# Constants built by GpSimd, and idle matmuls in more TensorE gaps, in an attention and mixer kernel

## The chip, the cores and the metric

The kernel runs on one core of a Trainium2 chip, in one launch. The metric is the device time of that launch in microseconds (us). The engines are TensorE (PE, with its weight loads shown apart as PEld), VectorE (DVE), ScalarE (ACT), GpSimd (POOL) and SyncE (SP, which here only issues transfers). Matmul results land in PSUM, which has eight banks; everything else lives in SBUF.

## What is computed

The inputs are q, k and v of 4 batches, 8 heads, 768 positions and 64 features, and four weight matrices. The attention is block-sparse: keys are split into 12 blocks of 64, each query takes the three best blocks by a gate (query times mean key of the block) and its own block, under a causal mask. A token and channel mixer follows.

```python
k_rep = k.reshape(B, H, n_blocks, block, D).mean(axis=3)
gate_scores = np.einsum('bhsd,bhnd->bhsn', q, k_rep)
gate_scores = np.where(causal, gate_scores, -1000000000.0)
top_idx = np.argsort(gate_scores, axis=-1)[..., -top_k:]
...
scores = scale * np.matmul(q, k.transpose(0, 1, 3, 2))
mask = mask & (pos[:, None] >= pos[None, :])
scores = np.where(mask, scores, -1000000000.0)
...
return np.matmul(attn, v).astype(np.float32)
...
h = np.maximum(xt @ w_tok1, 0.0) @ w_tok2
u = x + h.transpose(0, 2, 1)
h2 = np.maximum(u @ w_ch1, 0.0) @ w_ch2
return (u + h2).astype(np.float32)
```

## The kernel before

The 32 heads are handled as 16 pairs; a pair `i` is one batch and two neighbouring heads `x` = 0 and 1. For each pair `prepare(i)` loads k and q (L312, two transfers each on SP's queue), transposes them on TensorE against a float32 identity `ident32` (L356, tiles `tkl` and `tql`), and writes the fp16 operands `KA` and `QA` of the score matmul. Most of these casts run on GpSimd (`cast`, L376); those of pair 0 run on ScalarE (`direct` L385, `qact` L390). VectorE sums the keys of a block (`ksum` L395, `kcopy` L403), TensorE makes the gate scores (`gate`, L413, ten matmuls, tile `gps`), VectorE picks the best three (`gm`, `top`, `below`, `bias`, L452 to L498), and the resulting mask is transposed back (`mask`, L500) and copied into 24 more rows of `QA` (`put_mask`, L509).

The mask reaches the scores without an operation of its own: rows 64 to 87 of `KA` hold an indicator, a 1 where a key column belongs to block n of head x, so that the score matmul over 88 rows adds the penalty that stands in the same rows of `QA`. The indicator is a constant. Ring slot 0 of `KA` gets it by a transfer on ScalarE's queue (L969), the other four slots by one transfer on GpSimd's queue (`more_ind`, L337).

`attend(i)` (L817) then runs, for each head, three groups of score matmuls (`scores`, L516, tile `sps`), the exponentials on ScalarE (`expo`, L534), the causal diagonal, the product with V (`av`, L550, 21 matmuls into the tile `aps`), and on VectorE the reciprocal of the row sums (`recip`, L562) and the scaling into `x16` (`norm`, L570). The causal diagonal of pair 0 is added on TensorE, by a matmul of `ident16` with a triangle `tri` (L530); of all other pairs VectorE multiplies by a 0/1 triangle `m0` (`diag`, L542). `tri` is made from `m0` by GpSimd (`make_tri`, L341), and `m0` and `ident32` come by transfer (L970, L947). PSUM is shared out as two tiles of two banks (ring `big`: transposes and scores), three single banks (ring `bank`) and one bank for the product with V (ring `av`). When the four pairs of a batch are through, its mixer follows (`tok1`, `umix`, `ch1`, `ch2`), mixed in between the attention of later pairs.

The order of the work is made by a planner. Every piece is an `Op` with an engine, an estimated occupancy and duration, its dependencies, a priority and the buffers it takes. `plan` (L118) goes forward in planned time, gives each engine the ready piece of best priority among those that can start within 60 ns of the earliest, and returns one list; the program issues the pieces in this order, and each engine runs its share strictly in it. The planner's start times per engine are in `free` (L121). The framework adds the semaphore waits that the data call for. Those for PSUM go by bank: two engines are kept apart in one bank even where their columns differ or both only read.

Idle matmuls are pieces like others (`dummy`, L706): a matmul of a zero tile `warm` on itself, without dependencies, with the worst priority (IDLE). The planner puts one wherever TensorE would otherwise wait, as long as planned time has not passed `WARM_END` (17,000 ns) and the `WARM` = 120 of them are not used up. They are 256 columns wide, are planned at 213 ns for the first `COLD` = 20 and 109 ns after, and write a tile that holds the slot of the ring `av`.

What stands ahead of the planned list: VectorE clears `warm`, ScalarE loads the exponential and starts the transfer of `ident32`, VectorE casts it to `ident16` and clears tiles, GpSimd sets the ones in V, starts the transfer of `m0` and clears the tiles `bn` (L944 to L972).

Of the kernel before, what the change touches and what calls it, by code (L numbers as in the profile page):

```python
# [9 lines left out]
FP = mybir.dt.float32  # L10
# [18 lines left out]
R = 5  # L29
# [3 lines left out]
EARLY = 1  # L33
UVIA = 1
LEAD = 960.0
WARM, COLD, WARM_END = 120, 20, 17000.0
IDLE = 1e9
EXTRA = 5.0

# [78 lines left out]
def plan(ops, rings, near=60.0):  # L118


    free = dict(PE=900.0, ACT=4800.0, DVE=4500.0, POOL=4800.0, SP=750.0, SPO=750.0)  # L121
    slots = {name: [(0.0, None)] * n for name, n in rings.items()}
    moves = []
    casts = []
    waiting = {}
    users = {}
    ready = {e: [] for e in free}
    done = {}
    for op in ops:
        n = 0  # L130
        for d in op.deps:
            users.setdefault(id(d), []).append(op)
            n += 1
        waiting[id(op)] = n
        if n == 0:
            ready[op.eng].append(op)

    def finish(op, eng):
        return done[id(op)] + (LAT.get(eng, 33) if op.size == 0 else 60)

    def buf_free(buf, eng):
        t = 0.0
        for u in buf.users:
            if id(u) not in done:
                return None
            t = max(t, finish(u, eng))
        return t

    order = []
    left = len(ops)  # L150
    while left:
        best = None
        for o in [o for o in ready["PE"] if o.prio == IDLE and free["PE"] > WARM_END]:
            ready["PE"].remove(o)
            done[id(o)] = free["PE"]
            left -= 1
        if not left:
            break
        for e, cand in ready.items():
            if not cand:  # L160
                continue
            lst = []
            if e == "SP":
                if any(x.eng == e and x.prio < min(c.prio for c in cand) for x in ops if id(x) not in done):
                    continue
                cand = [min(cand, key=lambda c: c.prio)]
            for op in cand:
                t = free[e]
                for d in op.deps:
                    t = max(t, finish(d, e))  # L170
                ok = True
                for buf in op.takes:
                    first = None
                    for s, (_, old) in enumerate(slots[buf.ring]):
                        f = 0.0 if old is None else buf_free(old, e)
                        if f is not None and (first is None or f < first[0]):
                            first = (f, s)
                    if first is None:
                        ok = False
                        break  # L180
                    t = max(t, first[0])
                    buf.slot = first[1]
                if ok:
                    lst.append((t, op))
            if not lst:
                continue
            t0 = min(t for t, _ in lst)
            pick = min((x for x in lst if x[0] <= t0 + near), key=lambda x: (x[1].prio, x[0]))
            if best is None or pick[0] < best[0]:
                best = pick  # L190
        assert best is not None, "the plan cannot go on"
        t, op = best
        op.start = t
        for buf in op.takes:
            slots[buf.ring][buf.slot] = (0.0, buf)
        wait = 0.0
        if op.eng == "POOL" and not op.size:
            casts = [(t, t + op.rec)]
        elif op.two and casts and casts[0][0] <= t < casts[0][1]:
            wait = (casts[0][1] - t) % (450.0 if casts[0][1] - casts[0][0] > 900 else 1e9)  # L200
        free[op.eng] = t + op.occ + wait
        if op.eng in ("SP", "SPO"):
            free["SP"] = free["SPO"] = t + op.occ
        if op.size:
            moves.append((t + (1500 if op.eng == "POOL" else 1250), op))
            for o, d in transfers(moves).items():
                done[id(o)] = max(done.get(id(o), 0.0), d)
            now = min(free.values())
            moves = [(a, o) for a, o in moves if done[id(o)] > now - 2000]
        else:  # L210
            done[id(op)] = t + op.rec + wait
        ready[op.eng].remove(op)
        order.append(op)
        left -= 1
        for u in users.get(id(op), []):
            waiting[id(u)] -= 1
            if waiting[id(u)] == 0:
                ready[u.eng].append(u)
    return order, max(done.values())
# [3 lines left out]
def kernel(  # L223
# [19 lines left out]
    NFC = DC // 128  # L243
    scale = 1.0 / (D ** 0.5)
    MASKV = -30000.0
    GJ = NJ - 1

    sp = ctx.enter_context(tc.tile_pool(name="sb", bufs=1))
# [4 lines left out]
    RINGS = dict(big=2, bank=3, av=1, ql=3, kl=3, qt=4, kt=2, gs=1, gt=1, gm=1, m8=1, bn=NBN, e0=3, e1=3, e2=3, rc=2,  # L253
                 x16=2, h1=2, u=2, uT=2, h2=1, ob=3)

    def const(name, a, dt, eng):
        t = sp.tile(list(a.shape), dt, tag=name, name=name)
        eng.dma_start(out=t, in_=nc.inline_tensor(a, name=name + "c").ap())
        return t

    def sb(tag, shape, dt, name):
        return sp.tile(shape, dt, tag=tag, bufs=RINGS[tag], name=name)

# [3 lines left out]
        return pp.tile(shape, dt, tag=tag, bufs=RINGS[tag], name=name)  # L267


    V16 = [sp.tile([128, 2, NJ, 65], F16, tag=f"V{r}", name=f"V{r}") for r in range(R + 1)]  # L270
    MK = 64 + 2 * NB
    QAX = sp.tile([128, R, 2, S], F16, tag="QA", name="QA")
# [11 lines left out]
    gown = sp.tile([128, 3 * GJ * NB], FP, tag="gown", name="gown")  # L284
    gone = gown[:, 0:GJ * NB].rearrange("p (j n) -> p j n", n=NB)
    own = gown[:, GJ * NB:].rearrange("p (j c) -> p j c", c=2 * NB)
    ident16 = sp.tile([128, 128], F16, tag="id16", name="id16")
    tri = sp.tile([128, 128], F16, tag="tri", name="tri")
    m0 = sp.tile([128, 128], F16, tag="m0", name="m0")
# [44 lines left out]
    def twice(t):  # L334
        return t.rearrange("p j (x n) -> p j x n", x=1).broadcast_to([128, GJ, 2, NB])

    def more_ind():  # L337
        nc.gpsimd.dma_start(out=KAX[64:MK, 1:R],
                            in_=consts["ind"].rearrange("q (r x) s -> q r x s", r=1).broadcast_to([2 * NB, R - 1, 2, S]))

    def make_tri():  # L341
        nc.gpsimd.tensor_scalar(out=tri, in0=m0, scalar1=1.0, scalar2=-MASKV, op0=ALU.subtract, op1=ALU.mult)

    def own_four():
        for c in range(4):
# [203 lines left out]

    def av(i, x):  # L550
        def f():
            p = ps("av", [128, NJ, 65], "aps")
            T["aps", i, x] = p
            for jq in range(NJ):
                for kk in range(jq + 1):
# [149 lines left out]

    def dummy(n):  # L706
        def f():
            if n == 0:
                T["warm"] = ps("av", [128, NJ, 65], "warm").rearrange("p a b -> p (a b)")[:, 0:256]
            nc.tensor.matmul(out=T["warm"], lhsT=warm[:, 0:128], rhs=warm, start=True, stop=True)  # L710
        return f

    O = {}
    wb = Buf("av")
    for n in range(WARM):
        wb.users.append(pe(213 if n < COLD else 109, [], IDLE, dummy(n), [wb] if n == 0 else []))
    wq = []
    w1 = moe_w_tok1.rearrange("(j p) t -> p j t", p=128)
    w2 = moe_w_tok2.rearrange("(g p) s -> p g s", p=128)
# [97 lines left out]
    def attend(i):  # L817
        b, h = pairs[i]
        base = 10.0 * i
        for x in range(2):  # L820
            for g in range(3):
                pr = base + 3 * x + g
                big = Buf("big")
                occ = (434, 434, 271)[g] + (112 if i < TRI else 0)
                O["sc", i, x, g] = pe(occ, [O["put", i, x], O["cast", "kt", i, x], O["cast", "qt", i, x]] + ([ind_op] if 0 < i < R else []), pr,
                                      scores(i, x, g), [big])
                eb = Buf(f"e{g}")
                O["ex", i, x, g] = act(GROUPS[g][0], [O["sc", i, x, g]], pr, expo(i, x, g), [eb])
# [17 lines left out]
            ab.users.append(O["norm", i, x])  # L846

    op("SP", 950, 0, [], -36.85, load_gate_consts, size=400)
    op("POOL", 200, 250, [], -20.0, make_tri)
    ind_op = op("POOL", 600, 0, [], -9.0, more_ind, size=900)  # L850
    own_op = op("POOL", 960, 1000, [], 30.0, own_four)
    for G in GROUPED:
        for i in G:
# [3 lines left out]

    for i in range(6):
        O["v", i].deps.append(O["tr", "ql", i])
    ind_op.deps.append(O["gate", 0])  # L860
    for n, (at, f) in enumerate(wq):
        W.append(op("POOL", 700, 0, [O[("cast",) + WAIT[n]]], at, f, size=3200 if n < 2 else 2100))

# [78 lines left out]


    with tc.manual_schedule():  # L944
        nc.vector.memset(warm, 0.0)
        nc.scalar.activation(out=spare, in_=warm[:, 0:8], func=AF.Exp)
        ident32 = const("id32", np.eye(128, dtype=np.float32), FP, nc.scalar)  # L947
        pidx = np.arange(128)
        nidx = np.arange(NB)
        jidx = np.arange(1, NJ)  # L950
        mrow = 2 * jidx[None, :, None] + (pidx[:, None, None] >= 64)
        gb1 = (-1.0e6 * np.maximum(0, nidx[None, None, :] - mrow)).astype(np.float32)
        own1 = np.where(nidx[None, None, :] == mrow, 0.0, MASKV).astype(np.float32)
        ind1 = (np.arange(S)[None, :] // 64 == nidx[:, None]).astype(np.float16)
        ind_np = np.zeros((2, NB, 2, S), np.float16)
        for x in range(2):
            ind_np[x, :, x, :] = ind1
        ind_np = ind_np.reshape(2 * NB, 2, S)
        m0_np = (np.arange(128)[None, :] >= np.arange(128)[:, None]).astype(np.float16)
        ind_dram = nc.inline_tensor(ind_np, name="indc").ap()  # L960
        consts.update(ind=ind_dram, gown=nc.inline_tensor(np.concatenate(
            [gb1.reshape(128, -1), np.concatenate([own1, own1], axis=2).reshape(128, -1)], axis=1), name="gownc").ap())
        nc.vector.tensor_copy(out=ident16, in_=ident32)
        for r in range(R):
# [1 line left out]
        nc.vector.memset(QAX[64:MK, :, :, 0:128], 0.0)  # L966
        for r in range(R + 1):
            nc.gpsimd.memset(V16[r][:, :, :, 64:65], 1.0)
        nc.scalar.dma_start(out=KAX[64:MK, 0], in_=ind_dram)  # L969
        nc.gpsimd.dma_start(out=m0, in_=nc.inline_tensor(m0_np, name="m0c").ap())  # L970
        for y in range(NBN):
            nc.gpsimd.memset(bn16[y].bitcast(FP), 0.0)  # L972

# [35 lines left out]
```

## Time and profile before

| What | Value |
|---|---|
| Median of 6 runs | 272.24 us (270.55, 271.25, 271.31, 273.17, 273.65, 273.78) |
| The profiled execution | 273.78 us |
| Its span, first to last instruction | 271.9 us |
| PE busy | 261.1 us, 96% |
| DVE, ACT, POOL busy | 156.6, 145.2, 70.1 us |
| Idle matmuls in the trace (L710) | 58, of which 17 before the first transpose |
| Last idle matmul begins | 19.6 us |
| Mean granted TensorE clock | 0.981 |

The profiled execution is the longest of the six, and its time is 1.9 us above its span. Line numbers such as L710 are those of the kernel before. In the views quoted below, a row of the windows view gives the stretch, its length, then the busy time and number of instructions of PE, PEld, DVE, ACT and POOL, the share of full speed that the TensorE clock was granted, the share of the transfer engines, and GB/s. A row of the chain of waits gives start, length and the work that the end hung on. A row of the timeline gives start, length, engine, line and operation, and in brackets the idle time before it and what ended it.

### The profile page before, as it was taken

How to read it: one execution, taken by the hardware profiler on the slowest of the kernel's cores; microseconds unless marked ns; L12 is line 12 of the kernel's file. 1: busy time of each engine (PE TensorE's matmuls, PEld its weight loads, DVE VectorE, ACT ScalarE, POOL GpSimd, SP SyncE). 2: the span in 40 equal slices, each digit the busy share in tenths (PEclk: the TensorE clock that was granted, in tenths of full speed). 3: DMA queues.
4: the chain of work that ended last, by engine and by line, in shares of the span. 5: the costliest groups of instructions: out<-in, count | busy, mean ns of one | idle time of the engine just before them, and what ended most of it. 6: DMA issues, size and time to landing. Idle time of an engine off the chain costs nothing.

```text
span 271.9 us, 5694 instructions
## 1 busy us (share of the span) xinstructions
PE 261.1 (96%) x2226; PEld 166.2 (61%) x2226; DVE 156.6 (58%) x533; ACT 145.2 (53%) x194; POOL 70.1 (26%) x108
## 2 busy tenths in 40 slices
PE   7899899999999899999999999999999999999995
PEld 5777577887467667546575666664456544466443
DVE  1476756899496657997456985375333252333222
ACT  2747767866789684577766499890014410044100
POOL 4485923693632753223223000000000000000000
PEclk9999759999999999999999999999999999999999
DMA  8999999999999994716920000006330008220032
GB/s 172 205 177 201 196 188 197 174 191 194 202 194 126 188 188 86 105 39 121 94 81 17 23 2 0 2 2 115 120 115 0 0 9 187 77 77 2 0 122 109
DMA packets 91613, 29.22 MB, mean 107 GB/s; under 512 B 84972, under 2 KB 88044, under 8 KB 91588
## 3 DMA queue, kind: packets, MB, share of 16 engines
q1 hardware_dynamic: 63232, 21.33, 38.4%
q0 software_dynamic: 28176, 7.41, 26.8%
q8 instruction: 17, 0.28, 0.4%
q10 hardware_dynamic: 180, 0.14, 0.2%
q14 instruction: 8, 0.07, 0.1%
HBM read 27.30 MB, written 6.29 MB: 124 GB/s over the span
## 4 chain that ended last, share of the span: by engine, by line
PE 85%; DVE 7%; ACT 4%; issue 2%; POOL 1%; DVEq 0%; ACTq 0%; POOLq 0%
PE c L691 23%; PE c L670 22%; PE sps L526 13%; PE aps L558 7%; PE tkl L362 4%; PE tok L589 3%; PE ups L601 3%; PE tql L362 2%; DVE kst L400 2%; PE warm L710 2%; PE gps L418 2%; ACT kt L373 2%; PE gtp L428 1%; PE tok L620 1%; PE bps L506 1%
## 5 line engine op out<-in xcount | busy, mean ns | idle before, releaser
L539 ACT ACTIVATE e<-sps 128x1024 f16<-128x1024 f32 (+1 forms) x96 | 84.4, 918 | 17.7 <-PE sps L526 16.1
L670 PE MATMUL c<-uT,wc 128*128 128x256 f16 (+1 forms) x384 | 68.4, 326 | 0.0
L691 PE MATMUL c<-wc,h 128*128 128x512 f16 (+2 forms) x300 | 65.5, 370 | 0.0
L680 ACT ACTIVATE h<-c 128x512 f16<-128x512 f32 x48 | 28.7, 598 | 59.4 <-PE c L670 41.2
L526 PE MATMUL sps<-QA,KA 88*128 88x512 f16 (+3 forms) x256 | 52.0, 318 | 2.6 <-POOL QA L382 0.8
L670 PEld LDWEIGHTS <-wc 128*128 128x128 f16 x384 | 36.7, 98 | 22.8
L691 PEld LDWEIGHTS <-h 128*128 128x128 f16 x300 | 28.8, 98 | 30.9 <-issue 0.8
L526 PEld LDWEIGHTS <-KA 88*128 88x128 f16 x256 | 23.2, 102 | 22.1 <-issue 2.9
L546 DVE TENSOR_TENSOR e<-e,m 128x256 f16<-128x256 f16 x90 | 27.4, 313 | 16.1 <-ACT e L539 15.3
L682 DVE TENSOR_SCALAR h<-c 128x256 f16<-128x256 f32 x48 | 20.2, 421 | 28.5 <-PE c L670 28.3
L699 DVE TENSOR_TENSOR ob<-u,c 128x512 f32<-128x512 f16 (+2 forms) x25 | 16.6, 666 | 34.2 <-PE c L691 34.2
L382 POOL CAST QA<-qt 64x768 f16<-64x768 f32 x30 | 25.2, 841 | 14.5 <-ACT qt L373 13.1
L558 PEld LDWEIGHTS <-e 128*128 128x128 f16 x672 | 26.1, 100 | 3.3 <-issue 0.4
L558 PE MATMUL aps<-V,e 128*128 128x65 f16 x672 | 27.5, 197 | 0.0
L326 POOL DMA_DIRECT2D V<-in_v_dram x16 | 16.4, 1027 | 17.5 <-PE aps L558 16.8
L382 POOL COPY KA<-kt 64x384 f32<-64x384 f32 x24 | 12.2, 508 | 32.6 <-ACT kt L373 17.8
L577 DVE TENSOR_TENSOR x<-aps,rc 128x384 f16<-128x384 f32 x32 | 17.7, 554 | 0.7
L400 DVE TENSOR_REDUCE kst<-tkl 128x12 f32<-128x768 f32 x13 | 12.4, 954 | 8.1 <-ACT kt L373 5.4
L373 ACT COPY qt<-tql 128x768 f32<-128x768 f32 x16 | 12.8, 801 | 7.8 <-PE tql L362 7.8
L362 PE MATMUL tkl<-id,kl 128*128 128x128 f32 x96 | 14.1, 285 | 1.2 <-DVE kst L400 0.6
L512 DVE COPY QA<-bps 24x640 f16<-24x640 f16 x32 | 14.3, 481 | 1.2 <-PE bps L506 0.8
L362 PE MATMUL tql<-id,ql 128*128 128x128 f32 x96 | 13.5, 277 | 0.7 <-ACT e L539 0.3
(65 smaller groups left out, 214.0 us busy)
## 6 DMA issues: line engine op xcount, KB each, us to landing
kl<-in_k_dram SPq DMA_DIRECT2D x32, 192.0 KB, 5.1
ql<-in_q_dram SPq DMA_DIRECT2D x32, 192.0 KB, 5.2
out_dram<-ob SPq DMA_DIRECT2D x23, 256.0 KB, 2.0
V<-in_v_dram POOLq DMA_DIRECT2D x16, 192.0 KB, 6.7
wc<-in_moe_w_ch_dram POOLq DMA_DIRECT2D x8, 384.0 KB, 8.4
w<-in_moe_w_tok_dram POOLq DMA_DIRECT2D x2, 384.0 KB, 8.0
KA<-indc POOLq DMA_DIRECT2D x1, 288.0 KB, 8.1
out_dram<-ob SPq DMA_DIRECT2D x1, 160.0 KB, 1.8
```

Source lines behind the costliest of these rows:

```text
L362: nc.tensor.transpose(out=p[:, 128 * j:128 * j + 128], in_=t[:, j, :], identity=ident32)
L373: nc.scalar.copy(out=t, in_=p[:, 0:S])
L382: nc.gpsimd.tensor_copy(out=to, in_=src)
L400: nc.vector.tensor_reduce(out=kst, in_=kt.rearrange("p (n w) -> p n w", w=64), axis=AX.X, op=ALU.add)
L526: nc.tensor.matmul(out=p[:, off + a:off + a + n], lhsT=KA[i % R][x][0:MK, 128 * kk:128 * kk + 128], rhs=QA[i % R][x][0:MK, q0 + a:q0 + a + ...
L539: nc.scalar.activation(out=e[:, 0:width], in_=T["sps", i, x, g][:, 0:width], func=AF.Exp, scale=scale)
L546: nc.vector.tensor_tensor(out=d, in0=d, in1=m0.rearrange("p (a b) -> p a b", a=1).broadcast_to([128, 2, 128]), op=ALU.mult)
L558: nc.tensor.matmul(out=p[:, jq, :], lhsT=T["e", i, x, g][:, o:o + 128], rhs=V16[i % (R + 1)][:, x, kk, :], start=(kk == 0), stop=(kk == jq))
L670: nc.tensor.matmul(out=p, lhsT=wc1_16[:, cc, 128 * fc:128 * fc + 128], rhs=T["uT", b][:, cc, a // 128:e // 128, :], start=(cc == 0), stop= ...
L680: nc.scalar.activation(out=T["h2", b][:, fc, a:e], in_=T["c1", b, fc, n], func=AF.Relu)
L682: nc.vector.tensor_scalar(out=T["h2", b][:, fc, a:e], in0=T["c1", b, fc, n], scalar1=0.0, scalar2=None, op0=ALU.max)
L691: nc.tensor.matmul(out=T["c2", b, j, lo], lhsT=T["h2", b][:, fc, 128 * j:128 * j + 128], rhs=wc2_16[:, fc, lo:hi], start=(fc == 0), stop=( ...
```

## The change

- `ident32` is no longer transferred. VectorE fills it with ones, and GpSimd keeps the diagonal with `affine_select`. `m0` and `tri` are made by `affine_select` too, `m0` from a tile of ones and `tri` from the zeros in `warm`.
- The indicator is no longer transferred. For each ring slot GpSimd multiplies a stretched-out 24 x 24 corner of `ident32` by a float32 number that is two fp16 ones side by side. Slot 0 is done ahead of the planned list, slots 1 to 4 are planned pieces of 860 ns, and the scores of pairs 1 to 4 each depend on that of their own slot.
- The two helpers `more_ind` and `make_tri` go, and with them four transfers: 64 KB and 72 KB on ScalarE's queue, 32 KB and 288 KB on GpSimd's.
- The bank of the ring `av` becomes one tile `avp`, allocated once. `av` uses its columns 0 to 389, and the idle matmuls its columns 390 to 511. They are 122 columns wide, planned at 107 ns for the first 40 and 54 ns after, up to 300 of them, and up to a planned time of 46,000 ns.
- The planner takes GpSimd as free from 5,200 ns instead of 4,800.

```diff
-WARM, COLD, WARM_END = 120, 20, 17000.0
+WARM, COLD, WARM_END = 300, 40, 46000.0
...
-    free = dict(PE=900.0, ACT=4800.0, DVE=4500.0, POOL=4800.0, SP=750.0, SPO=750.0)
+    free = dict(PE=900.0, ACT=4800.0, DVE=4500.0, POOL=5200.0, SP=750.0, SPO=750.0)
...
+    ONES = float(np.array([1.0, 1.0], np.float16).view(np.float32)[0])
...
+    avp = pp.tile([128, 512], FP, tag="av", bufs=1, name="avp")
...
+    ident32 = sp.tile([128, 128], FP, tag="id32", name="id32")
...
-    def more_ind():
-        nc.gpsimd.dma_start(out=KAX[64:MK, 1:R],
-                            in_=consts["ind"].rearrange("q (r x) s -> q r x s", r=1).broadcast_to([2 * NB, R - 1, 2, S]))
-
-    def make_tri():
-        nc.gpsimd.tensor_scalar(out=tri, in0=m0, scalar1=1.0, scalar2=-MASKV, op0=ALU.subtract, op1=ALU.mult)
+    def indicator(r):
+        nc.gpsimd.tensor_scalar(out=KAX[64:MK, r].rearrange("q x s -> q (x s)").bitcast(FP).rearrange("q (m w) -> q m w", w=32),
+                                in0=ident32[64:MK, 64:MK].rearrange("q (m w) -> q m w", w=1).broadcast_to([2 * NB, 2 * NB, 32]),
+                                scalar1=ONES, scalar2=None, op0=ALU.mult)
...
-            p = ps("av", [128, NJ, 65], "aps")
+            p = avp[:, 0:65 * NJ].rearrange("p (j c) -> p j c", c=65)
...
-            if n == 0:
-                T["warm"] = ps("av", [128, NJ, 65], "warm").rearrange("p a b -> p (a b)")[:, 0:256]
-            nc.tensor.matmul(out=T["warm"], lhsT=warm[:, 0:128], rhs=warm, start=True, stop=True)
+            nc.tensor.matmul(out=avp[:, 390:512], lhsT=warm[:, 0:128], rhs=warm[:, 0:122], start=True, stop=True)
...
-    wb = Buf("av")
     for n in range(WARM):
-        wb.users.append(pe(213 if n < COLD else 109, [], IDLE, dummy(n), [wb] if n == 0 else []))
+        pe(107 if n < COLD else 54, [], IDLE, dummy(n))
...
-    op("POOL", 200, 250, [], -20.0, make_tri)
-    ind_op = op("POOL", 600, 0, [], -9.0, more_ind, size=900)
+    ind_op = [None] + [op("POOL", 860, 900, [], -20.0 + r, lambda r=r: indicator(r)) for r in range(1, R)]
...
-    ind_op.deps.append(O["gate", 0])
...
+        nc.vector.memset(ident32, 1.0)
+        nc.gpsimd.affine_select(out=ident32, in_=ident32, pattern=[[-1, 128]], compare_op=ALU.is_equal, fill=0.0,
+                                base=0, channel_multiplier=1)
         nc.vector.memset(warm, 0.0)
+        nc.vector.memset(m0, 1.0)
         nc.scalar.activation(out=spare, in_=warm[:, 0:8], func=AF.Exp)
-        ident32 = const("id32", np.eye(128, dtype=np.float32), FP, nc.scalar)
+        indicator(0)
+        nc.gpsimd.affine_select(out=tri, in_=warm[:, 0:128], pattern=[[1, 128]], compare_op=ALU.is_ge, fill=MASKV,
+                                base=0, channel_multiplier=-1)
+        nc.gpsimd.affine_select(out=m0, in_=m0, pattern=[[1, 128]], compare_op=ALU.is_ge, fill=0.0,
+                                base=0, channel_multiplier=-1)
...
-        nc.scalar.dma_start(out=KAX[64:MK, 0], in_=ind_dram)
-        nc.gpsimd.dma_start(out=m0, in_=nc.inline_tensor(m0_np, name="m0c").ap())
```

More of the change, by code (lines that the diff above doesn't have):

```diff
@@ L254 @@
                  x16=2, h1=2, u=2, uT=2, h2=1, ob=3)
[L256 to L259, printed above, removed]
     def sb(tag, shape, dt, name):
@@ L824, in attend @@
                 occ = (434, 434, 271)[g] + (112 if i < TRI else 0)
-                O["sc", i, x, g] = pe(occ, [O["put", i, x], O["cast", "kt", i, x], O["cast", "qt", i, x]] + ([ind_op] if 0 < i < R else []), pr,
+                O["sc", i, x, g] = pe(occ, [O["put", i, x], O["cast", "kt", i, x], O["cast", "qt", i, x]] + ([ind_op[i]] if 0 < i < R else []), pr,
                                       scores(i, x, g), [big])
@@ L953 @@
         own1 = np.where(nidx[None, None, :] == mrow, 0.0, MASKV).astype(np.float32)
[L954 to L961, printed above, removed]
+        consts.update(gown=nc.inline_tensor(np.concatenate(
             [gb1.reshape(128, -1), np.concatenate([own1, own1], axis=2).reshape(128, -1)], axis=1), name="gownc").ap())
```

## The prediction

> **What bounds the kernel now.** I read the page first. TensorE is busy for 96% of the span, so its time is the kernel's, and the clock row falls in slices 5 to 7 (each 6.8 us).
>
> ```profile
> PE 261.1 (96%) x2226; PEld 166.2 (61%) x2226; DVE 156.6 (58%) x533; ACT 145.2 (53%) x194; POOL 70.1 (26%) x108
> PEclk9999759999999999999999999999999999999999
> ```
>
> Then the windows view, cut finer until the edges of the fall were found, and once for the stretch where TensorE works without a gap.
>
> ```profile
> 20.56:23.97 3.41, 3.18 (x34) 2.41 (x32) 1.78 (x9) 2.55 (x3) 2.46 (x3) 1.00 1.64 195
> 27.39:30.80 3.41, 2.83 (x32) 1.94 (x28) 2.92 (x16) 2.15 (x3) 3.37 (x5) 1.00 1.34 217
> 30.80:34.21 3.41, 2.87 (x19) 1.59 (x20) 2.45 (x9) 2.82 (x4) 3.35 (x5) 0.50 1.65 172
> 37.63:41.04 3.41, 3.41 (x37) 2.79 (x35) 1.54 (x5) 2.12 (x4) 1.03 (x1) 0.50 1.60 173
> 41.04:44.45 3.41, 3.41 (x53) 2.84 (x52) 1.93 (x6) 2.86 (x5) 0.00 (x0) 1.00 1.12 202
> ```
>
> ```profile
> 31.35:41.04 9.69, 9.69 (x78) 6.45 (x79) 5.40 (x16) 6.29 (x8) 4.09 (x5) 0.50 1.45 184
> ```
>
> The granted clock is half from 30.80 to 41.04, 10.24 us, and TensorE is busy throughout its last 9.69. The stretch just before has the smallest busy share of the rows at full clock. Last the start: the chain of waits up to 9 us, the transfers issued before 5.4 us, and GpSimd's groups.
>
> ```profile
> 4.87 0.58 issue
> 5.45 1.53 PE tkl L362 x6
> 6.99 0.80 ACT KA L387
> 7.82 0.97 DVE kst L400
> 8.81 0.80 ACT KA L387
> ```
>
> ```profile
> kl<-in_k_dram SPq DMA_DIRECT2D x4, 192.0 KB, 4.1
> KA<-indc ACTq DMA_DIRECT2D x1, 72.0 KB
> id<-id32c ACTq DMA_DIRECT2D x1, 64.0 KB, 3.0
> m<-m0c POOLq DMA_DIRECT2D x1, 32.0 KB, 4.3
> ```
>
> The transposes begin at 5.45, after 0.58 us in which nothing on an engine releases them. The second half of k was issued at 1.25; plus 4.1 us that is 5.35, so k is what they wait for. Identity landed at 1.04 + 3.0 = 4.04, earlier.
>
> **The change, part by part.**
>
> *The clock.* What fell short before 30.80 can be put in streamed columns. Score matmuls follow one another at 512 columns in 0.22 us, 2.33 columns per ns. In 27.39 to 30.80 there are 2,688 columns of scores, 14 x 65 of AV and 10 x 24 of the gate: 3,838, or 1.65 us of 3.41, 48%. In 20.56 to 23.97, after which the clock held, the same count (with 6 x 128 of the triangle, 5 x 128 of the mask) gives 4,661, 59%. So I infer that the clock asks for something between 48 and 59%. TensorE's idle time in the later stretch is 0.28 (before the gate at 28.52) and 0.30 (30.50 to 30.80); filled with idle matmuls it would reach 1.65 + 0.58 = 2.23 us, 65%. That is enough.
>
> What the fall costs: 9.69 us of gapless TensorE at half clock would take 4.85 at full, a gain of 4.85 at most. ScalarE has 6.29 us of work in it, which leaves 9.69 - 6.29 = 3.40 if it becomes the bound there. The six times also stand in two groups, 270.55 to 271.31 and 273.17 to 273.78, 2.5 us apart in the mean; if the upper group are the executions with a fall, that is its price. Bounds 2.5 and 4.85; I take 3.0, near the two lower figures.
>
> The Trainium skill (TensorE: Matmul & The Clock Gate, "Why this matters for your kernels") says that the clock goes back to half after an idle gap of about 3 us. Here the largest gap before the fall was 0.84 us and not yet over. By the rule no filler was needed in gaps this short and this term would be 0, a sum near 273.7; I go by the row.
>
> *The start.* Three transfers, 168 KB, leave the time before k lands; up to 5.4 us 0.84 MB moved in about 3.6 us, 233 GB/s, so at most 0.72 us. They went on other queues and engines not wholly full, so at least 0.2. I take 0.5. The chain above (transposes, casts, block sums, gate, mask) moves with it one for one up to the first scores at 15.85, since ScalarE's next piece, `qt`, waits in ScalarE's own order. The transfer of 288 KB at 9.64 goes too; TensorE never waited for a transfer after 5.45, so 0. ScalarE's queue loses two issues (0.35 and 0.64 us), GpSimd's two (0.70 and 0.63); SP's keeps all.
>
> *GpSimd.* The nearest rows:
>
> ```profile
> L382 POOL CAST KA<-kt 64x768 f16<-64x768 f32 x2 | 1.6, 823 | 3.2 <-ACT kt L373 3.1
> L342 POOL TENSOR_SCALAR tri<-m 128x128 f16<-128x128 f16 x1 | 0.7, 662 | 2.3 <-DMA m<-m0c 2.3
> ```
>
> Identity comes first now. Before, GpSimd's configuration for L342 was issued at 3.30 and that instruction ended at 6.39, so both take 3.09 us at most; begun at 0.73, and after a clear of 0.17, identity is there by 4.0. The transposes want it at about 4.9: cost 0, with 0.9 us of cover. `tri` and `m0` take 0.66 each, wanted at 16.07 and 29.34. An indicator writes 768 float32 numbers per partition. Below: the cast of 768 columns, 0.82. Above: L342's 0.66 for 128 columns, six times over, 4.0. I take 0.9, since it is one pass over as many columns as the cast. Sum: 4.0 + 0.9 + 1.3 + memsets 0.42 and 1.31 + 4 x 0.9 + the copies for `own` 1.24 + the issue of V 1.11 = 13.9. Pair 1's casts began at 13.37 and would begin at 12.9: 1.0 late. They end at 15.08, and GpSimd next waits for `qt` until 16.55, 1.5 us of slack: cost 0. The new wait of each pair's scores on its slot is met as early.
>
> The Trainium skill (GPSIMD Engine Reference, "Instruction dispatch") puts the first call of a freshly loaded kernel at about 6 us. By that, identity would be there near 6.9 and the first transposes 1.5 us later than now, so that the start would lose what I let it win; the trace shows 3.09 at most.
>
> *VectorE.* Two more clears ahead of `warm`, 0.17 us each by its row at L945, behind the wait for k: 0.
>
> *The idle matmuls.* Up to 17 us of planned time the same time is filled in smaller pieces. The small matmul next to it, the 128-column triangle, follows at 0.06 us, against 0.054 planned. After that, TensorE's real gaps up to 48 us sum to some 3 us, about 50 idle matmuls. In a real gap they cost nothing (below: 0). Where the plan sees a gap that is not there, each costs 0.06: at most 50 x 0.06 = 3 us. Before, five of them ran from 19.33 to 19.88 while the path went through them, 0.55 us. I take 0.4.
>
> Their bank is also read by VectorE after each AV. The program keeps engines apart by bank: VectorE's block sum began at 7.82, right after ScalarE's cast of the same tile, though both only read. So an idle matmul that stands behind `norm` in the order waits for its end, with all of TensorE's queue behind it, the gate or the next transposes above all. Below 0, if gaps do not fall between AV and `norm`; above, 2.1 us (rival 2). I take 0.
>
> Sum, against the profiled execution: 273.78 - 3.0 - 0.5 + 0.4 = 270.7. That execution is the longest of six and stands 1.5 above their median; executions like the lower three have no 3.0 to win, so all would end near 270.7.
>
> **The rivals.**
>
> *1. The gain is whole.* The 4.85 comes back, the start gives 0.7, the filler costs 0.2: 273.78 - 5.35 = 268.4. For it: TensorE is gapless over the 9.69 us, and mixer work of batch 0 follows at once. Against: ScalarE's 6.29 us, and the 2.5 us between the two groups.
>
> *2. Idle matmuls stuck behind `norm`: slower.*
>
> ```profile
> 27.65 0.60 PE L526 MATMUL sps<-QA,KA 88*128 88x512 f16 x3
> 28.52 1.27 PE L418 MATMUL gps<-ks,qt 128*128 128x24 f32 x10 [0.28 <-DVE ks L408]
> ```
>
> The gap before 28.52 lies between an AV that ended at 27.65 and its `norm`, which ended at 29.20; filled, it becomes a stall of 0.68. The gap before 46.18 lies ahead of a `norm` that ends at 47.61, a stall of 1.43. Together 2.1; and as the first leaves 28.5 to 29.2 unfilled, the clock can fall as before and 2.5 to 3.0 is not won. 270.7 + 2.1 + 3.0 = 275.8. It decides (over 275.0) if the stalls and the lost gain pass 4.3 us. Against: the plan may put other work there.
>
> *3. The filler does not hold the clock.* The plan's gaps lie elsewhere than the real ones: 273.78 - 0.5 + 0.4 = 273.7.
>
> *4. Indicators near 4.0 us.* Five cost 16 us more. Pair 1's scores begin at 27.65 and its operands were ready at 18.25, 9 us of slack: 7 us late, 277 or more. It decides from about 2.6 us each on. Against: the cast's 0.82.
>
> **How the numbers follow.** One per cent, about what a measurement of this kernel can tell from no change, is 2.7 us: 269.5 and 275.0. Forecast 0.50 (own range 269.2 to 272.3); rival 1 0.19, rival 2 0.11, rival 3 0.14, rival 4 0.06. Faster by over 1%: rival 1 and 0.08 of the forecast, 0.27. Slower by over 1%: 0.10 of rival 2 and rival 4, 0.16. Within: 0.57. The range leaves out half of rival 1 below and some 0.11 above: 268.2 to 275.2.
>
> **What would show it.** Right: a granted clock of 1.00 from 7 us on in the windows; idle matmuls in the timeline between 28 and 31; `tkl` beginning near 4.9; indicator rows below 1 us. Wrong: a stretch at 0.50 again; PE rows at L706's matmul that wait for `norm`; `tkl` waiting for GpSimd; pair 1's casts beginning after 15.

## The result, and the profile after

The changed kernel took 271.35 us in the median of 37 runs (271.09 to 272.14), beside 271.38 for the kernel before in 79 runs (269.95 to 277.76): a ratio of 0.999, 95% interval 0.9976 to 1.0003. That is no change. The profiled execution took 271.38 us with a span of 269.7.

Two things in its profile are as the change wants them, the clock and the start. The page's totals, clock row and the group of the idle matmuls (the last columns are busy us, mean ns, and the idle time before them with what ended it):

```profile
PE 259.5 (96%) x2340; PEld 169.3 (63%) x2340; DVE 157.4 (58%) x535; ACT 144.8 (54%) x194; POOL 79.5 (29%) x113
PEclk9999999999999999999999999999999999999999
L704 PE MATMUL avp<-warm 128*128 128x122 f16 x172 | 14.1, 240 | 2.9 <-DVE x L573 1.7
```

The clock row has no dip left. But TensorE's busy time fell by only 1.6 us, although the 10.24 us at half clock are gone: the idle matmuls are now 172, and 1.7 us of TensorE's idle time ends with VectorE's `norm` (`x`, L573). The windows show the stretch where the clock fell before:

```profile
27.39:30.80 3.41, 2.76 (x30) 2.30 (x29) 1.97 (x14) 1.69 (x3) 3.37 (x5) 1.00 1.32 225
30.80:34.21 3.41, 3.41 (x57) 2.71 (x55) 3.15 (x9) 2.96 (x4) 3.35 (x5) 1.00 1.73 189
37.63:41.04 3.41, 3.41 (x59) 2.96 (x59) 1.94 (x7) 3.17 (x6) 0.97 (x1) 1.00 1.43 206
```

The granted clock is 1.00 in all three. ScalarE's busy time in the last one rose from 2.12 to 3.17 us: with a faster TensorE it is fed better. POOL is busy for 3.37 and 3.35 of 3.41 us, which it was before as well.

The chain of waits (start, us, what) tells where the win was lost. First its start:

```profile
1.27 3.64 PE avp L704 x34
4.91 1.33 PE tkl L358 x6
6.26 0.80 ACT KA L383
7.08 0.97 DVE kst L396
```

The first transposes begin at 4.91 instead of 5.45, and the chain runs through TensorE's queue up to them. Then the stretch from the fourth gate to the first token-mixing matmul, `tok`:

```profile
27.72 0.08 PE avp L704
...
27.82 0.57 DVE x L573
...
28.43 0.21 PE avp L704
28.65 1.09 PE gps L414 x10
29.73 0.71 PE sps L522 x5
30.44 0.96 PE avp L704 x18
...
35.03 0.57 DVE x L573
...
35.65 0.53 PE avp L704 x7
...
37.56 0.27 PE avp L704 x2
37.83 0.67 PE tok L616 x12
```

Idle matmuls (`avp` L704) are links of the chain, before and after each `norm`: from 28.43 to 37.83 those in it sum to 2.8 us (with three shorter pieces of 0.16 to 0.38 that are left out above). So work waits for them here, and they wait for `norm`, whose bank they share. Not all of the 2.8 is lost; what it costs is measured below.

How much is lost can't be read against the profile shown of before, since that execution had the fall. For that the kernel before was profiled once more, below.

### The profile page after: what moved, and what is told of

Its sections match the earlier page's. It is cut to its first block, busy times and chain, and to the rows that moved or that the text cites. A ratio compares the mean times of both kernels' runs of the same rounds, so it can differ in the third digit from the quotient of the medians.

```text
span 269.7 us, 5929 instructions
## 1 busy us (share of the span) xinstructions
PE 259.5 (96%) x2340; PEld 169.3 (63%) x2340; DVE 157.4 (58%) x535; ACT 144.8 (54%) x194; POOL 79.5 (29%) x113
## 4 chain that ended last, share of the span: by engine, by line
PE 88%; DVE 5%; ACT 4%; issue 1%; DVEq 0%; ACTq 0%
PE c L687 23%; PE c L666 22%; PE sps L522 13%; PE avp L554 6%; PE tkl L358 4%; PE avp L704 4%; PE tok L585 3%; PE ups L597 3%; PE tql L358 3%; PE gps L414 3%; DVE kst L396 2%; ACT kt L369 1%; PE gtp L424 1%; PE bps L502 1%; DVE QA L508 1%
## 5 line engine op out<-in xcount | busy, mean ns | idle before, releaser
L522 PE MATMUL sps<-QA,KA 88*128 88x512 f16 (+3 forms) x256 | 49.5, 306 | 1.6 <-ACT qt L369 0.7
L678 DVE TENSOR_SCALAR h<-c 128x256 f16<-128x256 f32 x48 | 20.3, 422 | 28.5 <-PE c L666 28.2
L522 PEld LDWEIGHTS <-KA 88*128 88x128 f16 x256 | 22.3, 98 | 19.2 <-issue 0.9
L378 POOL CAST QA<-qt 64x768 f16<-64x768 f32 x30 | 25.2, 841 | 14.4 <-ACT qt L369 12.9
L554 PEld LDWEIGHTS <-e 128*128 128x128 f16 x672 | 25.1, 97 | 3.0
L554 PE MATMUL avp<-V,e 128*128 128x65 f16 x672 | 26.5, 193 | 0.0
L573 DVE TENSOR_TENSOR x<-avp,rc 128x384 f16<-128x384 f32 x32 | 17.7, 554 | 1.6 <-PE avp L704 1.0
L704 PE MATMUL avp<-warm 128*128 128x122 f16 x172 | 14.1, 240 | 2.9 <-DVE x L573 1.7
```

Source lines behind the costliest of these rows:

```text
L378: nc.gpsimd.tensor_copy(out=to, in_=src)
L522: nc.tensor.matmul(out=p[:, off + a:off + a + n], lhsT=KA[i % R][x][0:MK, 128 * kk:128 * kk + 128], rhs=QA[i % R][x][0:MK, q0 + a:q0 + a + ...
L554: nc.tensor.matmul(out=p[:, jq, :], lhsT=T["e", i, x, g][:, o:o + 128], rhs=V16[i % (R + 1)][:, x, kk, :], start=(kk == 0), stop=(kk == jq))
L678: nc.vector.tensor_scalar(out=T["h2", b][:, fc, a:e], in0=T["c1", b, fc, n], scalar1=0.0, scalar2=None, op0=ALU.max)
L704: nc.tensor.matmul(out=avp[:, 390:512], lhsT=warm[:, 0:128], rhs=warm[:, 0:122], start=True, stop=True)
```

## The experiments

The theory from these chains: (A) one chain runs through GpSimd's queue, which issues the transfer of the token-mixing weights behind its casts, and ends with their landing; (B) the other runs through TensorE's own queue with the idle matmuls and the waits for `norm`. Both end at `tok`, near 37 us; the change makes B the later one. Rivals: GpSimd's long indicators alone cost the win; the filler alone does; the clock was never worth 3.0.

**The kernel before, once more.** No edit.

> The kernel before, unchanged, to see what the fall of the clock is worth and how often it comes. Theory: the fall comes in a minority of its executions only (of the 79 shown with the result, 17 lie above 272.9 us), so most executions have a mean granted clock above 0.995 and stand near 271.2 us, those with a fall near 0.98 and 2.2 us higher; an execution without a fall has a span near 269.5 us. Rival: the fall comes in every execution, and the changed kernel lost 2 to 3 us of its gain elsewhere: then every execution shows a clock near 0.98.

Measured: 271.2 us (12 runs) beside 271.7 for another copy of the same kernel measured with it, ratio 0.9957 [0.9928, 0.9987]. The same program against itself thus differs by 0.4%, and every ratio below has to be read with that. The profiled execution took 270.8 us with a span of 268.9, and its clock held throughout. The same program's profile with the fall took 273.78 and 271.9: the fall costs 3.0. Its chain of waits before `tok`:

```profile
28.07 0.89 issue
28.96 8.00 DMA w<-in_moe_w_tok_dram
...
37.00 0.84 PE tok L620 x12
```

Here `tok` waits for the weights. They were issued at 28.96, behind GpSimd's casts, and took 8.00 us to land. So the changed kernel is ahead by 0.39 at the first transposes (4.91 against 5.30), by 0.07 at the fourth gate (28.49 against 28.56 in the timeline), and behind by 0.67 at `tok` (37.67 against 37.00 in the timeline; the chain counts from the end of the step before and has 37.83). From `tok` on the two run in step: their last mixing matmuls begin at 265.99 and 265.38, 0.61 apart. So, with the clock held, the span is decided by what happens up to `tok`.

The mean granted clock of each execution sorts the runs of the kernel before. Over 97 executions (two more, of 645 and 673 us, are left out): 46 held it (0.997 or more), mean 271.4 us; 38 were a little lower (0.990 to 0.996, one short fall), mean 271.7; 13 were below that, mean 274.0. The long fall is worth 2.6 us, but comes in about one execution in eight, so the median holds nothing of it. The execution profiled here, 270.8, is faster than the mean of those that held the clock, 271.4: the two traces show where the changed kernel loses, and the medians show that in sum it is level.

**The constants alone.** The changed kernel, with the filler cut back to where it ended before.

```
-WARM, COLD, WARM_END = 300, 40, 46000.0
+WARM, COLD, WARM_END = 300, 40, 17000.0
```

> The changed kernel, but its idle matmuls end at 17 us of planned time again; constants by GpSimd stay. Theory (idle matmuls after 17 us cost about as much as the earlier start gains): 270.3 to 270.9 us in executions without a fall of the clock, and falls come back in some, 2 us higher. Rival (the late casts on GpSimd, behind indicators of 2.16 us each, eat the start's gain): no faster than the changed kernel, 271.3 or above.

Measured: 270.96 us, ratio 0.9975 [0.9949, 1.0002]. Its chain:

```profile
26.19 0.82 POOL KA L378
27.07 0.82 POOL KA L378
27.89 0.95 POOL V L324
28.84 8.22 DMA w<-in_moe_w_tok_dram
...
37.10 0.84 PE tok L616 x12
```

And its wait (us in all, count, longest):

```profile
PE tok L616 <- DMA w<-in_moe_w_tok_dram: 1.7, 1, 1.7
```

With less filler TensorE is at `tok` 1.7 us early, at 35.40, and stands there until the weights land at 37.06. In the traces of this run and of the changed kernel TensorE's other matmuls come in the same order, and in the changed kernel it is at `tok` only at 37.83: the filler after 17 us, with its waits, makes chain B 2.4 us longer. So chain A takes over as soon as B gets shorter, and the span (269.1) is that of the kernel before (268.9): the start that was won is gone at 37 us. In 9 of the 12 executions the clock fell again, for a short time in seven and a long one in two.

**The filler alone.** The kernel before, with its constants still by transfer, and the new idle matmuls (the same bank, counts and end).

```
-WARM, COLD, WARM_END = 120, 20, 17000.0
+WARM, COLD, WARM_END = 300, 40, 46000.0
```

> The kernel before with the new idle matmuls alone; its constants still come by transfer. Theory: no fall of the clock in any execution, the start as before (first transpose near 5.45 us), and idle matmuls that wait for the scaling after AV: 271.3 to 272.3 us. Rival (GpSimd's indicators eat the gain of the idle matmuls): 270.0 to 270.8 us, faster than either kernel.

Measured: 272.87 us, 1.0049 [1.0023, 1.0075], above the expected range. In ten of twelve executions the clock held, at 272.83 in the mean. The kernel before's held ones, measured with it, have 271.65, and those of its second copy (the first experiment) 270.65, which is also a measure of the noise: the filler costs 1.2 to 2.2 us. The profiled execution had a fall of 3.41 us at 20.23, so the filler doesn't hold the clock always. It also waited 1.0 us for a load of q ahead of that, so its span does not price the filler.

**Idle matmuls that the plan keeps out of the bank's use.** The changed kernel; the planner is told that an idle matmul needs the AV bank free.

```
-        pe(107 if n < COLD else 54, [], IDLE, dummy(n))
+        pe(107 if n < COLD else 54, [], IDLE, dummy(n), [Buf("av")])
```

> The changed kernel, but the planner places an idle matmul only when the AV bank is free in its plan, so that none stands between an AV and its scaling. Theory (idle matmuls stuck behind the scaling cost 1 us or more before 29 us): TensorE's waits for the scaling (1.7 us) are gone, 270.2 to 270.9 us; the clock may fall in some executions, since the gap before the gate of pair 3 is open again. Rival (the stalls cost nothing, as TensorE would wait there for GpSimd's casts anyway): 271.2 to 271.6 us.

Measured: 272.7 us, 1.0007 [0.9966, 1.0048], from 270.7 (three executions that held the clock) over 272.5 (four with a short fall) to 274.2 (five lower). Only the first three lie in the expected range. In the profile the idle matmuls' waits for `norm` are down to one of 0.4 us, and TensorE came to `tok` early:

```profile
PE tok L616 <- DMA w<-in_moe_w_tok_dram: 1.9, 1, 1.9
```

Its own work ended at 35.15, 2.7 us before the changed kernel's 37.83. More than half of that is won by the fourth gate, as the expectation had it. From the timelines of the changed kernel, of the short filler and of this one:

```profile
28.43 0.21 PE L704 MATMUL avp<-warm 128*128 128x122 f16 x1 [0.65 <-DVE x L573]
28.49 1.25 PE L414 MATMUL gps<-ks,qt 128*128 128x24 f32 x10
```

```profile
26.74 1.25 PE L414 MATMUL gps<-ks,qt 128*128 128x24 f32 x10
```

```profile
26.96 1.25 PE L414 MATMUL gps<-ks,qt 128*128 128x24 f32 x10
```

TensorE's other matmuls come in the same order in all three. This kernel still has 28 idle matmuls between that gate and `tok`, and is there no later than the one with the short filler (35.40). So idle matmuls that do not wait for `norm` cost nothing here, and those that stand behind it cost 2.4 to 2.7 us at `tok`.

The windows show what followed (columns as above; 0.50 is the clock):

```profile
36.80:43.60 6.80, 6.51 (x59) 5.39 (x60) 1.24 (x4) 3.04 (x5) 0.00 (x0) 0.50 1.50 186
```

The wait for the weights ends at 37, and the clock is half from 36.80 on for 6.8 us. The wait for the weights was hidden by idle matmuls in the changed kernel; uncovered, it stands just ahead of a new fall. That it caused the fall is not shown: in the trace with the short filler the clock held through a wait of 1.7 us.

**Lighter indicators.** The changed kernel; GpSimd copies slots 1 to 4 from slot 0 instead of computing each.

```
 def indicator(r):
+    if r > 0:
+        nc.gpsimd.tensor_copy(out=KAX[64:MK, r]..., in_=KAX[64:MK, 0]...)
+        return
```

> The changed kernel, but slots 1 to 4 of the indicator are copied by GpSimd from slot 0, in the same order and with the same planned cost. Theory (the four planned indicators, 2.16 us each where 0.9 was assumed, keep GpSimd busy without a break from 5 to 31 us, so that the casts of pair 3 and behind them the transfer of the first mixer weight are late; that transfer is what the first mixer matmul waits for): a copy takes 0.8 to 1.0 us, the weight transfer is issued 1 us or more before 29.1, 270.2 to 270.9 us. Rival (the idle matmuls behind the scaling after AV set the pace): transfer earlier or not, 271.2 to 271.5 us.

Then the copies by VectorE, before the first pair:

```
+        nc.vector.tensor_copy(out=KAX[64:MK, r]..., in_=KAX[64:MK, 0]...)
-    ind_op = [None] + [op("POOL", 860, 900, [], -20.0 + r, ...) for r in range(1, R)]
+    ind_op = [None] * R
```

> The changed kernel, but slots 1 to 4 of the indicator are copied by VectorE ahead of the planned list, and GpSimd has no planned indicator. Theory (GpSimd's queue): 8.6 us of GpSimd gone, its busy share between 5 and 29 us below 0.75, the weight transfer issued before 28.0, 269.8 to 270.7 us. Rival (stalls behind the scaling): 271.2 to 271.5 us.

Measured: 271.61 us, 1.0 [0.998, 1.0021], and 272.01 us, 1.0016 [0.9996, 1.0035]. The groups of the changed kernel, then of the two (busy us, mean ns):

```profile
L336 POOL TENSOR_SCALAR KA<-id 24x768 f32<-24x768 f32 x5 | 10.7, 2132 | 0.4
L937 POOL TENSOR_SCALAR_AFFINE_SELECT id<-id 128x128 f32<-128x128 f32 x1 | 0.3, 291 | 0.6 <-DVE id L936 0.6
```

```profile
L337 POOL COPY KA<-KA 24x768 f32<-24x768 f32 x4 | 3.2, 825 | 0.1
```

```profile
L337 DVE COPY KA<-KA 24x768 f32<-24x768 f32 x4 | 2.7, 736 | 1.1 <-POOL KA L340 1.1
```

An indicator took 2.13 us, a copy of it 0.83 and 0.74. From 5 to 29 us GpSimd was busy for 23.07 of 24 us in the changed kernel, 18.34 and 16.69 in these two, 14.88 before. The weights were issued at 28.15 and 28.20 instead of 29.09. Yet the time did not fall, and `tok` began at 38.15 and 37.38. GpSimd's load is not what the changed kernel's time hangs on: that rival falls, and B is its bound.

**The weights earlier, by their place in the plan.** The changed kernel, and the one with VectorE's copies, with the weights' transfers made to follow the key casts of pair 2:

```
-WAIT = [("kt", 3, 1), ("kt", 3, 1), ("qt", 3, 1), ("qt", 3, 1), ("qt", 4, 1), ("qt", 4, 1),
+WAIT = [("kt", 2, 1), ("kt", 2, 1), ("qt", 3, 1), ("qt", 3, 1), ("qt", 4, 1), ("qt", 4, 1),
```

> The changed kernel with one edit: the transfers of the two token weights wait for the casts of pair 2 instead of pair 3. Indicators and idle matmuls stay. Theory (the first mixer matmul waits for the weight transfer): it is issued near 24 to 25 us, the weight lands before 34, mixer matmuls fill TensorE's gaps between 31 and 37 us in place of idle ones, 269.3 to 270.5 us. Rival (the weight's landing does not matter, as the casts and the scaling bind TensorE there): 271.0 to 271.6 us, or slower where the loads of pair 3 come later.

> Both edits of the two runs before: indicators copied by VectorE, and the token weights one pair earlier. If both theories on GpSimd's queue hold, the best of the four, 268.8 to 270.0 us, and faster than the kernel before by 0.6 to 1%. If the stalls behind the scaling bind, 271 us.

Measured: 278.14 us, 1.0212 [1.0164, 1.026] in six runs, and 272.82, 1.0059 [1.0031, 1.0087]. These two tell nothing about the weights. The plan is made anew from the edit, and the order moved everywhere (in the first, the transposes of pair 6 began at 60.4 instead of 53.0, and the weights were issued at 26.07 and still waited for, 1.5 us). From here on the transfers were moved in the finished order, with nothing planned anew.

**Less filler and lighter GpSimd.** VectorE's copies, and the filler cut back to 17000 as above.

> Constants by GpSimd and VectorE (indicator slots 1 to 4 copied by VectorE), idle matmuls only up to 17 us of planned time. The theory that GpSimd's indicators alone cost the gain fell in the two runs before. New theory: two chains reach the first mixer matmul at about 37 us, the transfer of the token weight (issued near 28 to 29, about 8 us to land) and TensorE's own queue with its idle matmuls; taking one away leaves the other. So here TensorE waits 1 to 2 us for the weight again and the time is as in the run with the short filler, 270.3 to 271.0 us, with falls of the clock in many executions. Rival (idle matmuls alone bind): 269.6 us or less, without a wait for the weight.

Measured: 272.43 us, 1.0003 [0.9968, 1.0037]; three executions held the clock, at 270.02 in the mean, and seven had a mean clock of 0.981 to 0.987, at 272.8. The profiled one had two falls of 3.41 us each, at 23.03 and 33.27, came to `tok` only at 38.96 and did not wait for the weights, so the wait that was expected is not seen.

**Chain A taken away.** Right after the plan is made:

```
+    for w in (W[1], W[0]):
+        order.remove(w)
+        order.insert(order.index(O["cast", "kt", 2, 1]) + 1, w)
```

It was put into three kernels: the last one (VectorE's copies, short filler), the kernel before with nothing else, and the kernel with VectorE's copies, the full filler and the idle matmuls kept out of the bank's use.

> As the run before it in this call, and the two token weights' transfers moved in the finished order to directly behind the key casts of pair 2, all else in the same order. Theory of the two chains: both are gone, TensorE does not wait for the weight, the first mixer matmul begins near 35 us, 269.0 to 270.0 us where the clock holds. Rival (a third chain, the casts and transposes of pairs 3 and 4, binds as late): mixer matmul earlier, but the transposes of pair 4 not before 40.3 us, 270.3 to 271.0.

> The kernel before with only that move of the two transfers. Theory: its chain of waits runs through the weight from 28.96 to 36.95 us, but TensorE's wait for it was 0.4 us in the execution without a fall, so not more than 0.4 to 0.8 us is won: 270.4 to 271.2. Rival (transfers of weights ahead of the loads of pair 3 delay those): 271.5 or slower.

> The changed kernel with indicator slots copied by VectorE, idle matmuls up to 46 us of planned time but placed only where the AV bank is free in the plan, and the move of the two transfers. Theory of the two chains: neither the weight nor stalls behind the scaling bind, and the remaining filler holds the clock; 269.0 to 270.2 us with few falls. Rival: falls of the clock come back as in the earlier run with the bank kept free, 271 to 273 us.

Measured, in that order: 268.95 us, 0.9882 [0.9858, 0.9905]; 270.95 us, 0.9958 [0.9933, 0.9984]; 269.73 us, 0.9923 [0.99, 0.9947]. The chain of the kernel before with the move, then of the third:

```profile
35.39 0.86 PE aps L558 x21
...
36.53 0.67 PE tok L620 x12
```

```profile
35.03 0.66 PE avp L558 x21
...
35.96 0.67 PE tok L620 x12
```

The weights were issued at 20.96 and 20.51, and from 20 us on no step of either chain is a transfer any more. In the kernel before TensorE's own work, with the exponentials it waits for, now reaches `tok` at 36.53, 0.47 earlier than the landing let it. That is the end of chain B in the kernel before; in the changed kernel it is 37.83. The 1.3 between them is not the filler's price, since the start and the order of the work differ too. The third kernel has neither the wait for the weights nor idle matmuls behind `norm`, and is at `tok` 1.87 us before the changed kernel; its span is 267.8, 1.9 shorter, and its clock held in all six executions.

The stretch from the fourth gate to `tok` (begin to begin, in the timelines) separates the two kinds of filler. It takes 9.18 or 9.19 us in all four kernels with idle matmuls behind `norm` (the changed one, the filler alone, both with copied indicators), 8.05 in the third kernel, which has the full filler but none behind `norm`, and 7.86 in the kernel before with the move. So in this stretch idle matmuls behind `norm` cost 1.1 us whatever makes the constants, and the others 0.2.

The first is the fastest, about 1.2% below the kernel before; four of its five executions held the clock, at 268.2 to 269.0, and one had two falls and took 273.0. The last is the profiled one, so no trace shows this kernel with the clock held. The kernel before with the move alone gained no more than the same program differed from itself (0.9957), so its median proves little; its trace, not its time, carries the reading above.

## Why the prediction was right and where it was not

The forecast of 270.7 lay 0.65 below the measured 271.35, which is inside its own range (269.2 to 272.3), and "within 1%" was its likeliest class. The sum came out near in part by luck: its largest term belongs to few executions, a term that was put at nothing costs 2.4 to 2.7 us of TensorE's work up to `tok`, and a wait that the sum does not have hides most of that.

- **The clock, −3.0.** The mechanism and the size held for the execution that was profiled: 273.78 with the fall, 270.8 without, same program. The step that failed here is the base. The working took the profiled execution and said that the others "have no 3.0 to win"; true, but those are seven in eight, and the kernel's median is theirs. Six times in two groups of three looked like an even mix, and in 97 executions it was 13 to 84. In the changed kernel the filler held the clock: none of its 38 executions listed was below 0.997. In two others with filler up to 46000 it did not always (two of twelve lower with the filler alone, nine of twelve with the bank kept free). The inference that the clock asks for 48 to 59% of streamed columns does not come out of the later traces. These are a stretch of the run with the short filler, then one of the fastest kernel's profiled execution and the stretch behind it:

```profile
22.21:25.62 3.41, 2.55 (x28) 2.02 (x25) 2.72 (x6) 2.02 (x3) 3.25 (x5) 1.00 1.30 191
```

```profile
20.39:23.80 3.41, 2.95 (x27) 2.13 (x25) 1.97 (x6) 2.37 (x3) 3.31 (x5) 1.00 1.78 192
23.80:27.21 3.41, 3.41 (x35) 2.94 (x32) 2.00 (x15) 1.40 (x2) 0.25 (x1) 0.50 1.37 200
```

Counted in the same way the first has 3,527 columns, 44%, and the clock held behind it; the second has 4,080, 51%, and the clock fell.
- **The start, −0.5.** Measured 0.54 against the profile of before (5.45 to 4.91), 0.39 against the one without the fall. Right. It was to move on "one for one" to the first scores; by the fourth gate 0.07 was left. The stalls behind `norm` had used it up: in the same order without most of them that gate came at 26.74 and 26.96.
- **The idle matmuls, +0.4 (bounds 0 and 3).** Apart from those behind `norm` the term was rather too high: TensorE reached `tok` at 35.15 with such filler and at 35.40 with the short one, and in the order of the kernel before it cost 0.2 us between the fourth gate and `tok`.
- **Behind `norm`, 0 (above: 2.1).** This step failed too: the term was left at nothing, on the chance that the plan puts other work there, and the mechanism of rival 2 came. The changed kernel's waits of TensorE:

```profile
PE avp L704 <- DVE x L573: 1.7, 3, 0.7
```

Three waits, 1.7 us in all, one of them ahead of the gate at 28.5 as the rival said, at 0.65 instead of 0.68. Behind a wait the idle matmuls still run ahead of other work (15 of them at 25.00, ahead of transposes that began at 25.80 here and at 25.18 with the bank kept free), and together this cost 2.4 to 2.7 us at `tok`, above the bound. Only some 0.6 of it reaches the span, since the weights land near 37.05 in any case. The rival's second half, that the clock would then fall, did not come, so the time stayed near 271.
- **What is late next.** "TensorE never waited for a transfer after 5.45" was read from the execution with the fall, in which TensorE came too late to wait for anything. It is the step that hid the second chain: without the fall it waits for the weights at 37 (0.4 us, and 1.7 or 1.9 with less filler). Any gain before 37 beyond some 0.4 us had nowhere to go.
- **GpSimd, 0.** The identity was ready by 1.44, not 4.0: the first select began at 1.15. The Trainium skill (GPSIMD Engine Reference, "Instruction dispatch") has some 6 us for the first call of a freshly loaded kernel; this trace shows none of that. An indicator was 2.13 us, not 0.9 (bounds 0.82 and 4.0, so they held; the cast of the same columns was the wrong row to lean on). Pair 1's casts began at 18.18 and not at 12.9, past the sign of 15 that was to prove the prediction wrong, and that cost nothing that shows: the run with GpSimd's copies began them at 12.60 and was no faster, so the 9 us of slack that rival 4 names took it up. Its point of decision, 2.6 us each, was just not reached.
- **The clock page's rule.** The Trainium skill (TensorE: Matmul & The Clock Gate, "Why this matters for your kernels") gives an idle gap of about 3 us for a fall. The traces here disagree: the largest gap ahead of a fall was 0.84 us in the kernel before and 1.9 us in the one with the bank kept free.

**What stays open.** Why the clock falls in some executions of one program and not in others; no run settles it. Why the lighter indicators by VectorE came out at 272.0 while its profile (271.6) has `tok` 0.45 earlier than the changed kernel. Its last mixing matmul still begins 0.47 earlier (265.52), but 4.36 us of its span follow, where every other trace has 3.56 to 3.90: in the profiled execution the lead is lost at the very end, and whether the others lost it there is not known. How much of the fastest kernel's gain is the weights' and how much the clock's: with the clock held, its 268.6 is 1.4 below the one without the move (270.02, three executions), which is also what the move gave the kernel before (270.40 beside 271.76), though the trace there has only 0.5 at `tok`, and two copies of the same program differed by 1.0 in such means.

## What to carry to other kernels

Before a stall is priced, profile an execution that lacks it: what the profile with the stall calls never late is often the next bound, here a transfer queued behind casts on GpSimd that landed at the same moment. Two chains that end together must both be shortened: either alone measured no more than the noise (0.9975 with the short filler, 0.9958 with the weights moved), both together 0.9923 and 0.9882, though falls of the clock take part in these times. Filler on an in-order engine is nearly free only where it waits for nothing (0 to 0.2 us here): in a bank that another engine reads, it turns a gap into a stall for everything behind it (2.4 to 2.7 us).

## What the runs showed of the hardware

- GpSimd on 24 partitions and 768 float32 columns: a multiplication by a constant with a broadcast input took 2.13 us, a plain copy 0.83 us; the copy by VectorE 0.74 us. A select by position over 128 x 128 took 0.29 us, less than half of the 0.66 us that a subtraction and multiplication in one instruction took on as many float16 elements before.
- The weights' transfer, issued by GpSimd at 29 while other loads ran, took 8.0 to 8.2 us to land.
- The clock's falls had lengths of 3.41, 6.83 and 10.24 us, which are one, two and three times the same length. The streamed columns of the 3.41 us ahead did not tell whether a fall came (none after 44%, one after 51%).
- The changed kernel's times lay closer together: a standard deviation of 0.24 us over its 38 executions, beside 0.76 over 41 of the kernel before that held the clock too. Before, the path goes through a transfer's landing, and after, it doesn't; that this is why was not tried.
